# Chunk-selected attention with top-1 routing: the order of TensorE's work in a head pair, and three score units on column tiles

## The chip, the cores and the metric

The kernel runs on one core of a Trainium2 chip. The metric is the device time of one execution in microseconds. The kernel before takes 360.15 us (median of three runs, 359.7 to 360.66). The engines are TensorE (PE; its weight loads are listed as PEld), VectorE (DVE), ScalarE (ACT), GpSimd (POOL) and SyncE (SP). TensorE reads SBUF and writes PSUM.

## The reference, cut to what matters

Attention over 4 batches of 8 heads, 768 positions and a head width of 64, in which every query attends only to its 6 best key chunks of 32 (and causally), followed by a layer of 8 experts in which every token goes to one expert.

```python
k_chunks = k.reshape(B, H, nc, chunk, D)              # nc = 24 chunks of 32 keys
k_min, k_max = np.min(k_chunks, axis=3), np.max(k_chunks, axis=3)
ub = np.sum(np.maximum(q[:, :, :, None, :] * k_min[:, :, None, :, :],
                       q[:, :, :, None, :] * k_max[:, :, None, :, :]), axis=-1)
ub = np.where(causal, ub, -1e9)
top_chunks = np.argsort(ub, axis=-1)[..., -6:]        # the selection
scores = scale * np.matmul(q, k.transpose(0, 1, 3, 2))
mask = sel & (pos[:, None] >= pos[None, :])           # sel: the key's chunk is among top_chunks
attn = softmax(np.where(mask, scores, -1e9))
x = attn @ v                                          # heads side by side: (3072, 512)

logits = x @ w_gate                                   # 8 experts
expert_idx = np.argmax(logits, axis=1)
out[token] = gate * (relu(x[token] @ w1[e]) @ w2[e])  # e = expert_idx[token]
```

The sum of the larger products is q·(k_max + k_min)/2 + |q|·(k_max − k_min)/2, so the kernel computes the bound by two matmuls, without the halves (the order stays the same).

## The kernel before

The kernel goes through 16 head pairs `i` (4 in a batch). Two heads are worked on together, side by side in the 128 partitions. For a pair, `prep_steps` transposes keys and queries, takes the smallest and largest of each key chunk, and makes the bounds, the selection and the mask rows, which are appended to the queries (`QSB`, rows 64 to 87) so that the score matmul adds -50 for every chunk not selected. The steps of pair i+1 and i+2 run inside pair i.

```python
def k_half(hf):                                   # hf: first or second half of the keys
    pt = ps_m.tile([128, 384], FP32, tag="m")
    for t in range(3):
        nc.tensor.transpose(pt[:, ts(t, 128)], s["k"][:, 3 * hf + t], ident_f[:])
    pk = pt[:].rearrange("p (c w) -> p c w", w=CH)
    nc.vector.tensor_reduce(s["kmx"][:, ts(hf, 12)], pk, AX.X, ALU.max)
    nc.vector.tensor_reduce(s["kmn"][:, ts(hf, 12)], pk, AX.X, ALU.min)
    nc.scalar.activation(kte[0:64, 0, ts(hf, 384)], pt[0:64, :], AF.Copy, bias=0.0, scale=0.125)
    nc.scalar.activation(kte[0:64, 1, ts(hf, 384)], pt[64:128, :], AF.Copy, bias=0.0, scale=0.125)
# q_t(hf): three transposes; q_e(hf): VectorE copy qT, ScalarE |q| (qA) and QSB of head 1
def kse():                                        # key sums and differences, block by head
    for hd in range(2):
        r = slice(64 * hd, 64 * hd + 64)
        c = slice(32 * hd, 32 * hd + NCH)
        nc.vector.tensor_tensor(ks[r, c], s["kmx"][r, :], s["kmn"][r, :], ALU.add)
        nc.vector.tensor_tensor(kd[r, c], s["kmx"][r, :], s["kmn"][r, :], ALU.subtract)
def ub():                                         # bounds: column tiles of 64
    for w_, nm in ((ks, "qT"), (kd, "qA")):
        for h in range(2):
            nc.tensor.matmul(pu[64 * h:64 * h + 64, 0:320], lhsT=w_[:], rhs=..., ...)
    nc.scalar.activation(s["ubT"][:, 0:320], pu[:, 0:320], AF.Copy)
# select(): three transposes of ubT, then on VectorE ubm, twelve MAX8, nsel
# mask():   six transposes of nsel into 64 partitions, two ScalarE copies into QSB
```

The scores of a pair come in seven units: 0 and 1 for the first half of the queries, 2 to 6 for the second. Unit 1 and unit 6 have two parts, 256 and 128 queries wide, the others one of 384. A score tile takes two PSUM banks, and there are two of them. The exponentials `P` go to the attention-times-V (AV) matmuls, which use column tiles of 64 (a head each), and are added up on VectorE for the softmax's denominator.

```python
ps_m = tc.alloc_tile_pool(name="ps_m", bufs=3, space=PSUM)   # transposes, bounds, sums
ps_s = tc.alloc_tile_pool(name="ps_s", bufs=2, space=PSUM)   # scores, 2 banks each
ps_o = tc.alloc_tile_pool(name="ps_o", bufs=1, space=PSUM)   # AV output

def scores(i, u):
    ...
    for n, (kb, w, c0) in enumerate(parts):
        for hd in range(2):
            nc.tensor.matmul(pv[:, hd, :], lhsT=kte[:, hd, ts(kb, 128)],      # 128 columns
                             rhs=qsb[:, hd, ds(qb * 384 + 384 - w, w)], ...)
    for pv, (kb, w, c0) in zip(pvs, parts):
        nc.scalar.activation(P[:, :, ds(c0, w)], pv, AF.Exp)                  # one for each part
    # affine_select on GpSimd for the diagonal blocks

def attend(i, u):
    if first: s["po"] = ps_o.tile([128, 384], FP32, tag="o", name="po")
    for n, (kb, w, c0) in enumerate(parts):
        for hd in range(2):
            nc.tensor.matmul(po[64 * hd:64 * hd + 64, 384 - w:384], lhsT=vt[:, kb, hd, :],
                             rhs=P[:, hd, ds(c0, w)], ...)
    if last:
        nc.vector.tensor_copy(out=ot[:], in_=po[:])
    # and on VectorE: acc += P, except for the first unit
```

The router's part of a pair: `ud` (column tiles of 32: the denominators and the logits), `lgp` (transposes of it, reciprocal, division), `x0` and `x1` (transposes of the outputs `ot`, scaling into rows). Once in a batch the tokens are ranked (`rank`). The program order of a pair is also the order of TensorE, GpSimd and SyncE; the order of VectorE and ScalarE inside the loop is picked by the compiler, with program order as the priority.

```python
for g in range(4):
    if g == 0:   scores(i, 2); scores(i, 3); run(rout, i - 2, "x1")
    elif g == 1: scores(i, 4); scores(i, 5)
                 if hp == 1 and b > 0: route[b - 1][1]()            # rank
                 run(prep, i + 1, "select")
    elif g == 2: scores(i, 6); run(prep, i + 2, "k0"); run(prep, i + 1, "mask")
    else:        run(rout, i - 1, "lgp", "x0")
                 scores(i + 1, 0); scores(i + 1, 1)
                 run(prep, i + 2, "k1", "q0", "q0e", "q1")
    for u in groups[g]: attend(i, u)          # groups = (0, 1), (2, 3), (4, 5), (6,)
    if g == 3: run(prep, i + 2, "q1e", "kse")
    if g == 0: run(prep, i + 1, "ub")
    if g == 1: run(rout, i - 1, "ud")
```

## Time and profile before

| what | value |
|---|---|
| time, median of three runs | 360.15 us |
| profiled execution, span | 358.6 us |
| first pair's preparation | to 16.6 us |
| loop, first score matmul of pair 0 to that of pair 15 | 16.58 to 230.70 us |
| a regular pair | 13.66 us |
| a pair that ranks a batch | 15.65 us |
| first expert matmul | 243.13 us |

Times in the profile are microseconds from the start of the span. "L298" is line 298 of the kernel. `128*64` behind a matmul is the part of the array that its weights take: 128 rows, 64 columns. An fp32 matmul shows as two instructions with the same shape, a bf16 one as one. TensorE's ends are modelled, so what counts is where the next group starts. "<-" names what ended a wait; "issue" means that nothing in the profile held the engine.

### The profile page before, as it was taken

What the parts mean: (1) busy time and instruction counts of PE and PEld (TensorE: products, weight loads), DVE (VectorE), ACT (ScalarE), POOL (GpSimd) and SP (SyncE); (2) the same over time, 40 slices, a digit from 0 to 9 for tenths busy, and PEclk for the clock granted to TensorE, in tenths of its full rate; (3) what the DMA queues carried; (4) which work ended last, traced back from release to release, by engine and by line L of the source; (5) the groups of instructions that cost most, each with busy time, mean ns of one, the idle gap of its engine ahead of it and who ended that gap; (6) DMA issues with size and microseconds to landing.
All of it is one profiled execution on the core that took longest, in us unless ns stands there. A gap on an engine that the chain in (4) does not pass through costs nothing. (4 is left out here: it accounts for less than half of the span.)

```text
span 358.6 us, 7585 instructions
## 1 busy us (share of the span) xinstructions
PE 326.9 (91%) x2312; PEld 171.5 (48%) x2312; DVE 235.0 (66%) x815; ACT 231.2 (64%) x398; POOL 180.4 (50%) x296
## 2 busy tenths in 40 slices
PE   6679999999899999999999988998799999999990
PEld 5535455455455465554554545443344344444430
DVE  5799889889999898999988999846460000000000
ACT  2497797797687897867977967642344444445440
POOL 3075425445474453466534547575577665653331
PEclk9999999999999999999999999999999999999996
DMA  8619998999957999937989973476999999998851
GB/s 153 112 26 194 210 220 139 215 167 215 207 127 151 182 176 195 202 100 178 200 134 212 187 148 113 73 135 116 165 211 233 221 237 197 203 186 201 157 126 48
DMA packets 138215, 59.83 MB, mean 167 GB/s; under 512 B 122811, under 2 KB 131005, under 8 KB 138176
## 3 DMA queue, kind: packets, MB, share of 16 engines
q1 hardware_dynamic: 119072, 29.52, 45.4%
q0 software_dynamic: 17536, 29.42, 42.0%
q10 hardware_dynamic: 1568, 0.39, 0.6%
q8 instruction: 21, 0.34, 0.4%
q14 instruction: 18, 0.15, 0.2%
HBM read 56.14 MB, written 10.51 MB: 186 GB/s over the span
## 5 line engine op out<-in xcount | busy, mean ns | idle before, releaser
L332 DVE TENSOR_TENSOR Pa<-Pa,Pr 128x768 f32<-128x768 f32 (+2 forms) x112 | 81.6, 729 | 1.1
L307 POOL TENSOR_SCALAR_AFFINE_SELECT Pr<-Pr 128x256 f32<-128x256 f32 x80 | 33.5, 437 | 67.3 <-ACT Pr L303 66.1
L303 ACT ACTIVATE Pr<-ps 128x768 f32<-128x768 f32 (+2 forms) x112 | 65.0, 630 | 3.2 <-PE ps L298 2.9
L612 PE MATMUL py<-w_all,hT 128*128 x224 | 52.7, 379 | 2.7 <-DMA hT<-h__3653 1.9
L298 PE MATMUL ps<-QSB,KTE 128*128 128x384 bf16 (+2 forms) x288 | 50.4, 292 | 1.2 <-DVE QSB L711 0.2
L620 POOL DMA_INDIRECT out_dram<-y,ti_all x28 | 27.8, 993 | 30.2 <-ACT y L619 26.3
L298 PEld LDWEIGHTS <-KTE 128*128 128x128 bf16 x288 | 24.1, 97 | 27.3 <-issue 21.2
L612 PEld LDWEIGHTS <-hT 128*128 128x128 bf16 x224 | 21.8, 98 | 29.5 <-DMA hT<-h__3653 2.3
L619 ACT ACTIVATE y<-py,gt_all 128x512 f32<-128x512 f32 x27 | 18.6, 687 | 20.8 <-PE py L612 18.4
L454 POOL DMA_INDIRECT xs_dram<-xrow,sli x24 | 26.9, 1121 | 7.7 <-issue 5.0
L356 ACT ACTIVATE ud<-pu 128x384 f32<-128x384 f32 x16 | 7.9, 492 | 32.8 <-PE pu L353 30.7
L303 ACT ACTIVATE Pa<-ps 128x768 f32<-128x768 f32 x32 | 26.0, 812 | 3.8 <-PE ps L298 3.2
L601 PE MATMUL ph<-w_all,KTE 128*128 x120 | 28.4, 379 | 0.0
L169 POOL DMA_DIRECT2D w_all<-in_moe_w_dram x32 | 24.3, 760 | 0.0
L307 POOL TENSOR_SCALAR_AFFINE_SELECT Pa<-Pa 128x256 f32<-128x256 f32 x16 | 6.4, 398 | 35.3 <-ACT Pa L303 35.3
L601 PE MATMUL ph<-w_all,QSB 128*128 x96 | 22.7, 379 | 0.3 <-issue 0.3
L575 DVE TENSOR_TENSOR ti_all<-xgqA,inv_i 128x1 int32<-128x1 int32 x9 | 1.4, 159 | 29.6 <-DMA xgqA<-xs_dram,grow 29.6
L554 POOL DMA_INDIRECT xgqA<-xs_dram,grow x14 | 14.6, 1046 | 10.2 <-issue 3.3
L554 POOL DMA_INDIRECT xgqT<-xs_dram,grow x14 | 14.5, 1033 | 8.7 <-DVE gt_all L577 4.9
L325 DVE COPY ot<-po 128x384 f32<-128x384 f32 x32 | 17.7, 553 | 1.6 <-PE po L320 0.9
L575 DVE TENSOR_TENSOR ti_all<-xgqT,inv_i 128x1 int32<-128x1 int32 x8 | 1.3, 159 | 26.5 <-DMA xgqT<-xs_dram,grow 26.5
L226 POOL CAST QSB<-qT 64x384 bf16<-64x384 f32 x30 | 16.3, 551 | 4.1 <-DVE qT L224 2.8
(311 smaller groups left out, 665.0 us busy)
## 6 DMA issues: line engine op xcount, KB each, us to landing
w_all<-in_moe_w_dram POOLq DMA_DIRECT2D x32, 512.0 KB, 6.0
out_dram<-y,ti_all POOLq DMA_INDIRECT x28, 3.6
t__122<-in_k_dram SPq DMA_DIRECT2D x2, 192.0 KB, 3.5
t__125<-in_q_dram ACTq DMA_DIRECT2D x2, 192.0 KB, 4.0
t__128<-in_v_dram SPq DMA_DIRECT2D x2, 192.0 KB
t__196<-in_k_dram SPq DMA_DIRECT2D x2, 192.0 KB, 3.1
t__206<-in_q_dram SPq DMA_DIRECT2D x2, 192.0 KB, 3.8
t__209<-in_v_dram SPq DMA_DIRECT2D x2, 192.0 KB
```

The costliest lines, as they stand in the source:

```text
L169: nc.gpsimd.dma_start(out=dst, in_=src.rearrange("(c p) f -> p c f", p=128))
L298: nc.tensor.matmul(pv[:, hd, :], lhsT=kte[:, hd, ts(kb, 128)], rhs=qsb[:, hd, ds(qb * 384 + 384 - w, w)], start=True, stop=True, skip_grou ...
L303: nc.scalar.activation(P[:, :, ds(c0, w)], pv, AF.Exp)
L307: nc.gpsimd.affine_select(out=pd, in_=pd, pattern=[[0, 2], [1, 128]], compare_op=ALU.is_ge, fill=0.0, base=0, channel_multiplier=-1)
L325: nc.vector.tensor_copy(out=ot[:], in_=po[:])
L332: nc.vector.tensor_tensor(acc[:, :, 384 - w:384], acc[:, :, 384 - w:384], P[:, :, ds(c0, w)], ALU.add)
L454: d = nc.gpsimd.indirect_dma_start(out=xs_dram[:], out_offset=bass.IndirectOffsetOnAxis(ap=sli[:, u:u + 1], axis=0), in_=bst[b][f"xrow{u % ...
L554: d = nc.gpsimd.indirect_dma_start(out=xg_bufs[j % XB].bitcast(I32), out_offset=None, in_=xs_dram[:], in_offset=bass.IndirectOffsetOnAxis( ...
L601: nc.tensor.matmul(ph[:, fh, :], lhsT=xT[:, c, :], rhs=w_all[:, ds(wo + (c * F + fh * 512), 512)], start=(c == 0), stop=(c == NDC - 1), sk ...
L612: nc.tensor.matmul(py[:], lhsT=hT[:, c, :], rhs=w_all[:, ds(wo + (W1W + c * DM), DM)], start=(c == 0), stop=(c == NFC - 1))
L619: nc.scalar.activation(y[:], py[:], AF.Copy, bias=0.0, scale=fs[j]["gt"])
L620: d = nc.gpsimd.indirect_dma_start(out=out[:], out_offset=bass.IndirectOffsetOnAxis(ap=fs[j]["ti"], axis=0), in_=y[:], in_offset=None, bou ...
```

## The change

TensorE's work in a pair is regrouped by the part of the array that it uses. Work on the full array (128*128) is to be done in two visits for each pair instead of four; all else goes on column tiles. For this, score units 2, 3 and 6, which stand between column-tiled work, are split over two column tiles of 64 keys each; the row transposes `x1` and the first key transposes `k0` move next to the selection's. To allow it, each step is taken apart into its TensorE (`_mm`), VectorE (`_v`) and ScalarE (`_a`) parts. With it come three smaller edits: the exponentials of a two-part unit become one instruction (the score tile is now laid out by head), the key sums and differences are made for both heads at once and multiplied by a 0/1 mask `bm` into one tile `KSD`, and the ranking's gate values are split from its logits.

```diff
-        def kse():
-            for hd in range(2):
-                r = slice(64 * hd, 64 * hd + 64)
-                c = slice(32 * hd, 32 * hd + NCH)
-                nc.vector.tensor_tensor(ks[r, c], s["kmx"][r, :], s["kmn"][r, :], ALU.add)
-                nc.vector.tensor_tensor(kd[r, c], s["kmx"][r, :], s["kmn"][r, :], ALU.subtract)
+        def kse():
+            kt2 = work.tile([128, 2, NCH], FP32, tag="top8", name="kt2")
+            nc.vector.tensor_tensor(kt2[:, 0], s["kmx"][:], s["kmn"][:], ALU.add)
+            nc.vector.tensor_tensor(kt2[:, 1], s["kmx"][:], s["kmn"][:], ALU.subtract)
+            nc.vector.tensor_tensor(ksd[:, :, :, 0:NCH], kt2[:].unsqueeze(2).to_broadcast([128, 2, 2, NCH]),
+                                    bm[:].unsqueeze(1).to_broadcast([128, 2, 2, NCH]), ALU.mult)
 ...
-    def scores(i, u):
+    def scores(i, u, split=False):
         ps = ps_s.tile([128, 2, 512], FP32, tag="s", name="ps")
+        n = 64 if split else 128
+        for kb, w, c0 in parts:
+            for hd in range(2):
+                for h in range(128 // n):
+                    nc.tensor.matmul(ps[ds(h * n, n), hd, ds(c0, w)], lhsT=kte[:, hd, ds(kb * 128 + h * n, n)],
+                                     rhs=qsb[:, hd, ds(qb * 384 + 384 - w, w)],
+                                     start=True, stop=True, skip_group_check=True)
-        for pv, (kb, w, c0) in zip(pvs, parts):
-            nc.scalar.activation(P[:, :, ds(c0, w)], pv, AF.Exp)
+        nc.scalar.activation(P[:], ps[:, :, 0:384], AF.Exp)
 ...                                      # the loop; n = i + 1, m = i + 2
                 if g == 0:
-                    scores(i, 2)
-                    scores(i, 3)
-                    run(rout, i - 2, "x1")
+                    scores(i, 2, True)
+                    scores(i, 3, True)
+                    av(i, 0)
+                    av(i, 1)
+                    o_ev(i, 0)
+                    add(i, 1)
+                    run(prep, n, "ub")
                 elif g == 1:
                     scores(i, 4)
                     scores(i, 5)
-                    if hp == 1 and b > 0:
-                        route[b - 1][1]()
-                    run(prep, i + 1, "select")
+                    run(prep, n, "sel_mm")
+                    run(rout, i - 2, "x_mm", 1)
+                    run(prep, m, "k_mm", 0)
+                    if router:
+                        rank_mm()
+                    run(prep, n, "sel_v")
+                    if router:
+                        rank_v()
+                    run(rout, i - 2, "x_v", 1)
+                    run(prep, m, "k_v", 0)
+                    run(prep, m, "k_a", 0)
+                    av(i, 2)
+                    av(i, 3)
+                    add(i, 3)
+                    run(rout, i - 1, "ud")
                 elif g == 2:
-                    scores(i, 6)
-                    run(prep, i + 2, "k0")
-                    run(prep, i + 1, "mask")
+                    scores(i, 6, True)
+                    run(prep, n, "mask")
+                    av(i, 4)
+                    av(i, 5)
+                    add(i, 4)
+                    add(i, 5)
                 else:
-                    run(rout, i - 1, "lgp", "x0")
-                    if i + 1 < NP:
-                        scores(i + 1, 0)
-                        scores(i + 1, 1)
-                    run(prep, i + 2, "k1", "q0", "q0e", "q1")
+                    run(rout, i - 1, "lgp_mm")
+                    run(rout, i - 1, "x_mm", 0)
+                    if n < NP:
+                        scores(n, 0)
+                        scores(n, 1)
+                    run(rout, i - 1, "lgp_v")
+                    run(rout, i - 1, "x_v", 0)
+                    run(prep, m, "k_mm", 1)
+                    run(prep, m, "k_v", 1)
+                    run(prep, m, "k_a", 1)
+                    for hf in range(2):
+                        run(prep, m, "q_mm", hf)
+                        run(prep, m, "q_v", hf)
+                        run(prep, m, "q_a", hf)
+                    av(i, 6)
+                    o_ev(i, 1)
+                    add(i, 6)
+                    run(prep, m, "kse")
```

`av`, `o_ev` and `add` are the three parts of `attend`: the matmuls, the copy of the output, the add. The pools keep their buffers: three for `ps_m`, two for `ps_s`, one for `ps_o`.

## The prediction

> **What bounds the kernel now.** I read the page's busy times first, then the busy time of each engine per head pair, then the waits in the steady stretch from 100 to 200 us, then TensorE's own timeline for one pair.
>
> ```profile
> span 358.6 us, 7585 instructions
> PE 326.9 (91%) x2312; PEld 171.5 (48%) x2312; DVE 235.0 (66%) x815; ACT 231.2 (64%) x398; POOL 180.4 (50%) x296
> ```
>
> The second half of the span is the expert stage, and the change doesn't touch it. So the 66% of VectorE is an average over two different stages. The attention loop has to be read by itself, in stretches that run from one pair's first score matmul to the next pair's (columns: stretch, its length, then busy time and count of PE, PEld, DVE, ACT, POOL, granted clock, DMA share, GB/s):
>
> ```profile
> 115.42:129.08 13.66, 13.58 (x110) 7.45 (x108) 12.62 (x40) 11.36 (x22) 5.57 (x12) 1.00 1.00 167
> 129.08:142.74 13.66, 13.58 (x110) 7.45 (x108) 12.62 (x40) 11.36 (x22) 6.32 (x13) 1.00 1.20 198
> 142.74:158.39 15.65, 14.24 (x122) 7.74 (x120) 15.06 (x58) 11.78 (x24) 8.33 (x14) 1.00 0.85 166
> ```
>
> A regular pair takes 13.66 us, equal to the last digit from pair to pair. A pair that also ranks a batch's tokens takes 15.65 us, and there are three of those. In a regular pair TensorE is never seen idle, while VectorE has about 1.0 us free, ScalarE 2.3 us and GpSimd over 7 us. In a ranking pair VectorE has 0.6 us free and is the bound. The waits in the stretch:
>
> ```profile
> ACT ud L356 <- PE pu L353: 12.0, 6, 2.7
> PEld L298 <- issue: 8.8, 28, 0.5
> PEld po L320 <- issue: 7.0, 40, 0.2
> DVE ubm L251 <- PE pt L249: 4.5, 6, 0.9
> PEld pu L241 <- ACT qA L225: 1.3, 5, 0.3
> ```
>
> VectorE and ScalarE wait for TensorE (0.75 and 2 us in a pair). TensorE's weight loads wait mostly for "issue", which means for nothing that the trace shows. So TensorE sets the pace of a regular pair, with VectorE close behind. The timeline tells what "issue" is:
>
> ```profile
> 130.98 0.87 PE L320 MATMUL po<-Pr,t__1666 128*64 128x256 f32 x8
> 131.78 0.82 PE L298 MATMUL ps<-QSB,KTE 128*128 128x384 bf16 x4
> 132.50 0.55 PE L386 MATMUL pt<-ident_f,ot 128*128 128x128 f32 x3
> 132.98 0.87 PE L320 MATMUL po<-Pa,t__1869 128*64 128x384 f32 x4
> 133.68 0.82 PE L320 MATMUL po<-Pr,t__1869 128*64 128x256 f32 x8
> 134.32 0.71 PE L241 MATMUL pu<-qT,KS 128*64 128x320 f32 x4
> 134.86 0.71 PE L241 MATMUL pu<-qA,KD 128*64 128x320 f32 x4
> 135.50 1.06 PE L298 MATMUL ps<-QSB,KTE 128*128 128x384 bf16 x4
> 136.41 0.55 PE L249 MATMUL pt<-ident_f,ubT 128*128 128x128 f32 x3
> ...
> 142.36 0.55 PE L386 MATMUL pt<-ident_f,ot 128*128 128x128 f32 x3
> 142.74 0.82 PE L298 MATMUL ps<-QSB,KTE 128*128 128x384 bf16 x6
> ```
>
> Read starts, not durations: ends of matmuls are modelled. The four qT matmuls and the four qA matmuls are the same work. The first group hands over to another 128*64 group after 0.54 us, the second to a 128*128 group after 0.64. Three row transposes take 0.38 us (142.36 to 142.74) ahead of 128*128 work and 0.48 (132.50 to 132.98) ahead of 128*64 work. So **a change of tile shape costs about 0.10 us**. The attention-times-V group of eight takes 0.80 us (130.98) with a switch on either side and 0.64 (133.68) with none.
>
> **What the Trainium skill says.** "TensorEngine Tiling (Array Packing)", Key Properties: changing the tiling mode, not just the tile, drains the engine. The trace agrees, with 0.10 us for each change. The same page, Restrictions, says that column tiling disables fast weight load. The split scores lose it; but the mask transposes, with 64-column bf16 loads, start 0.06 us apart here (six within 0.36), so I expect their loads to stay hidden behind matmuls of 0.16 us. "TensorE: Matmul & The Clock Gate", its first table: VectorE's and ScalarE's queues are strict FIFO, so an op that TensorE needs waits behind whatever was queued ahead of it. That matters below.
>
> **Part 1, the visits.** Counted in program order, a pair now changes shape nine times: scores and x1 (full), AV and bounds (64), scores and select (full), AV (64), sums (32), score 6 and first keys (full), mask and AV (64), rows, scores and transposes (full), AV (64). Afterwards it is six: scores 4, 5 with select, x1 and first keys (full), AV (64), sums (32), score 6 split with mask and AV (64), rows, scores and transposes (full), AV with scores 2, 3 split and AV and bounds (64). Three changes fewer at 0.10 us: **-0.30 us a pair**. The slow first load after a switch (0.37 against 0.32 us between the first two AV starts) goes with them, another -0.05 or so.
>
> **Part 2, the split.** Units 2, 3 and 6 get 8 more matmuls and 8 more loads. Two column tiles run side by side: in the AV groups the partner starts 0.007 us later. A score of 384 columns stays at 0.16 us. The 128-wide part of unit 6 takes 0.056 us and has two loads to hide: **0 to +0.1 us**.
>
> **Part 3, the moved transposes.** x1 (0.38 us without its switch) and the first keys (0.34) are moved, not removed: 0 for TensorE. What moves with them is 0.98 us of ScalarE copies (two of 0.49), 0.93 us of VectorE reductions and 0.47 us of row scaling, out of the crowded stretch ahead of the bounds and into the one after the selection, where ScalarE now waits 1.9 us for the sums. In that stretch the last score unit (the 1.06 at 135.50, where 0.82 is usual) waits 0.24 us for its score buffer, behind ScalarE's queue. That should mostly go: **-0.1 to -0.24**.
>
> **Part 4, smaller things.** The key sums: now two groups whose means are 0.347 and 0.289 us, two of each in a pair, 0.88 us from start to start where I followed them. Then two short ops (0.17) and one of 96 elements (0.25, as the 96-element lgt product takes here): -0.3 us of VectorE. The exponentials of units 1 and 6: 0.59 + 0.39 become one of 0.81, -0.17 each on ScalarE, off the path.
>
> TensorE's own sum: 13.66 - 0.35 - 0.17 + 0.05 = **13.2 us**.
>
> **Part 5, what takes some back.** There is one PSUM tile for the output (the pool `ps_o` has one buffer). The last AV of a pair fills it, VectorE copies it out, the next pair's first AV overwrites it. Today two score units and x1 (0.72 + 0.48 us) lie between. Afterwards only two split units, about 0.65 and no switch. The copy needs about 0.27 us for the last matmul to end, 0.05 for the signal, 0.56 for the copy and 0.1 for the signal back: 0.98 us from the last AV start, against about 0.75 until TensorE is there. **+0.2 us at least**, even if VectorE takes it up at once. In the new program order both query copies (0.47 each) stand ahead of it, where one stood behind it until now; if VectorE keeps them so, +0.5. Then comes the loop through VectorE. From the start of the selection to the end of the key sums VectorE works without a gap; 12.62 - 0.3 less the output copy and the add of unit 1 (0.47 + 1.0) leaves 10.85 us. From there the bounds (1.15), scores (0.67), selection transposes (0.38) and two signals (0.3) bring it to the next selection: 10.85 + 2.5 = **13.35 us**. I take 13.35 us for a regular pair, -0.3.
>
> **Ranking pairs** are bound by VectorE (15.06 of 15.65). The 0.3 us of the key sums come off, and the rank matmuls, today ahead of the selection's and waiting 0.54 us for their operand, go behind it: -0.5 each.
>
> **Sum.** 12 regular intervals x 0.3 + 3 ranking x 0.5 = 5.1 us. The first pair (16.6 us, with the constants for the key sums on GpSimd) and the expert stage, which starts when the loop ends, keep their length. 360.15 - 5.1 = **355.0 us**.
>
> **Rivals.**
> 1. *The switches are the gain and nothing takes their place*: 13.1 us a pair and 1.0 off a ranking pair, 15 x 0.55 + 1.2, about 350.5 us. For it: VectorE has 1.0 us free. Against: that time lies in one gap ahead of the selection, and the output copy isn't in it.
> 2. *The output copy and VectorE's order become the wait*: the copy is taken up one or two ops late (0.47 to 0.93), and the pair ends at 13.6 to 13.9 us: 359 to 363. For it: VectorE ran without a gap up to the output copy in the pair that I followed. Against: work is taken out ahead of it (0.93 of reductions).
> 3. *DMA becomes the bound*, since the share is already 1.0 to 1.2 in regular pairs: no gain, 359 to 360. Against: no engine waits for a transfer between 100 and 200 us, and keys and queries are loaded two pairs ahead.
>
> **Range and chances.** My number lies between rivals 1 and 2. The range 351.0 to 360.5 takes in most of rival 1 and half of rival 2. Over 2% faster means under 352.9, so 0.48 us off every pair, nearly all of rival 1: 0.22. Over 2% slower means over 367, nearly half a microsecond added to every pair: 0.08. Within 2%: 0.70.
>
> **What would show it.** Right: bounds-to-split-scores without "issue" loads and six changes a pair; split scores 0.16 us per pair of tiles; a new wait of TensorE for the output copy ahead of unit 0's AV, some 0.2 us; regular pairs at 13.2 to 13.5 us; ranking pairs near 15.1; expert stage unchanged in length. Wrong: split scores at twice the time (loads exposed), which adds 0.9 us a pair; the output copy late by an op or more; or the mask waiting for the selection because row scaling and key reductions went ahead of it on VectorE.

## The result, and the profile after

The changed kernel takes 378.72 us (median of four runs, 378.21 to 380.27), the kernel before 359.92 us on the same chip (358.9 to 360.66). The ratio is 1.053, with a 95% interval of 1.049 to 1.057. The change made the kernel 5% slower; the prediction was 1.4% faster. In the profiled executions 377.3 us stand against 358.6: **18.7 us to explain**.

The head of the page, and the busy times of stretches that run from one pair's first score matmul to the next pair's (columns as before). First a regular pair, then a ranking pair, then pair 0:

```profile
span 377.3 us, 7736 instructions
PE 331.9 (88%) x2430; PEld 180.4 (48%) x2440; DVE 240.1 (64%) x799; ACT 228.9 (61%) x366; POOL 188.7 (50%) x297
```

```profile
125.78:140.99 15.21, 13.87 (x117) 7.87 (x117) 13.07 (x39) 11.24 (x20) 6.15 (x13) 1.00 1.00 159
156.19:171.89 15.70, 14.43 (x128) 8.37 (x128) 14.77 (x55) 11.40 (x21) 8.00 (x15) 1.00 0.84 157
17.47:35.15 17.68, 12.46 (x86) 6.88 (x87) 13.61 (x42) 11.16 (x20) 8.29 (x22) 0.90 0.42 75
```

A regular pair takes 15.20 us instead of 13.66, and there are seven such intervals (10.8 us in all). Pair 0 takes 17.68 instead of 14.40 (+3.3). The two pairs that follow a ranking pair take +1.4 and +1.1, the loop starts 0.9 us later (it scatters by more than that from run to run), the last interval is 0.9 longer, and pair 1 0.1. Ranking pairs are as long as before (+0.05 each), and from the start of the last pair to the end it is 127.98 us against 127.88. These sum to 18.7.

No engine is full now. TensorE and VectorE both stand still for more than a microsecond in a pair. The waits of the loop from 100 to 200 us (us in total, times, longest):

```profile
ACT ud L365 <- PE pu L362: 21.4, 7, 3.3
...
DVE ubm L264 <- PE pt L258: 6.5, 5, 1.6
...
PE ps L303 <- ACT QSB L285: 3.2, 10, 0.4
...
PE po L329 <- DVE ot L341: 1.4, 4, 0.4
```

Each of TensorE, VectorE and ScalarE waits for another of the three. Such a ring of waits has no single bound; one has to walk around it. TensorE's timeline of the regular pair, its waits in brackets:

```profile
126.50 0.65 PE L303 MATMUL ps<-QSB,KTE 128*128 128x384 bf16 x5 [0.40 <-ACT QSB L285]
...
128.29 0.87 PE L329 MATMUL po<-Pr,t__1463 128*64 128x256 f32 x8
128.99 0.82 PE L303 MATMUL ps<-QSB,KTE 128*64 128x384 bf16 x8
130.18 0.87 PE L329 MATMUL po<-Pa,t__1700 128*64 128x384 f32 x4 [0.37 <-POOL lg L391]
...
134.10 0.49 PE L400 MATMUL px<-ident_f,ot 128*128 128x128 f32 x3
134.43 0.49 PE L205 MATMUL pk<-ident_f,t__1855 128*128 128x128 f32 x3
135.28 0.87 PE L329 MATMUL po<-Pa,t__1700 128*64 128x384 f32 x4 [0.36 <-DVE ot L341]
...
140.29 0.49 PE L400 MATMUL px<-ident_f,ot 128*128 128x128 f32 x3
140.99 0.32 PE L303 MATMUL ps<-QSB,KTE 128*128 128x384 bf16 x1 [0.21 <-ACT QSB L285]
```

Compare each gap between starts with the same gap where nothing waited. The next pair's scores lose 0.37 (head 0) and 0.56 us (head 1, 0.72 from start to start instead of 0.16): the mask rows are copied late. The first AV loses 0.54, the AV after the selection 0.43, the bounds 0.19, the last score unit 0.15. That is 2.24 us, so TensorE's own work is 15.20 - 2.24 = **13.0 us**. The work shrank as predicted, and waits took the room. The "POOL lg" at the first AV is a name to be careful with: the output copy on VectorE ended 0.1 us before that AV started (130.08), and an experiment below moves the AV with the copy.

VectorE from the end of one pair through the selection to the key sums, in the kernel before; the prediction judged this stretch by busy time alone:

```profile
121.59 0.55 DVE L325 COPY ot<-po 128x384 f32<-128x384 f32 x1
...
123.33 0.46 DVE L251 TENSOR_TENSOR ubm<-pt,cbias 128x288 f32<-128x288 f32 x1 [0.86 <-PE pt L249]
123.83 1.12 DVE L259 MAX8 top<-ubm 128x8 f32<-128x24 f32 x12
...
133.97 0.17 DVE L234 TENSOR_TENSOR KD<-kmx,kmn 64x24 f32<-64x24 f32 x1
```

And after:

```profile
134.31 0.46 DVE L264 TENSOR_TENSOR ubm<-pt,cbias 128x288 f32<-128x288 f32 x1 [1.64 <-PE pt L258]
134.68 0.55 DVE L341 COPY ot<-po 128x384 f32<-128x384 f32 x1
135.14 1.10 DVE L272 MAX8 top<-ubm 128x8 f32<-128x24 f32 x12
136.17 0.54 DVE L405 TENSOR_TENSOR xrow<-px,rec 128x384 bf16<-128x384 f32 x1
...
137.46 0.54 DVE L211 TENSOR_REDUCE kmn<-pk 128x12 f32<-128x384 f32 x1
137.92 3.07 DVE L337 TENSOR_TENSOR Pa<-Pa,Pr 128x768 f32<-128x768 f32 x3
...
146.47 0.26 DVE L223 TENSOR_TENSOR KSD<-kt,bm 128x96 f32<-128x96 f32 x1
```

Look at the output copy. Before, it ran at 121.59, ahead of the selection, in the time in which VectorE waits for the bounds. After, it runs behind the selection's first op, and in front of it VectorE is idle for 1.64 us. The copy writes a tile `ot` (three buffers, two used in a pair), and the buffer it needs is still read by the x1 transposes of the pair before last. They now run at 134.10 on TensorE, behind the selection's transposes; the last AV into the output had started at about 131.5, some 3 us ahead of the copy. So the copy waits for x1, falls into VectorE's full stretch, and the AV that overwrites the output waits for the copy. From selection to the end of the key sums it was 10.81 us; now it is **12.43**. The rest of the ring is 2.85 and 2.77 us: 13.66 and 15.20.

The list of the difference, from start to start: output copy +0.46, x1's row scaling +0.46 (before it came after the key sums), the three long adds 2.99 instead of 2.72, reciprocal and first part of the add of unit 6 1.17 instead of 0.69, the second part of that add 0.67 instead of 0.46, key sums 0.78 instead of 0.87, query copies -0.14, the selection's first op -0.13.

ScalarE around its one long gap:

```profile
138.03 0.49 ACT L365 ACTIVATE ud<-pu 128x384 f32<-128x384 f32 x1 [2.95 <-PE pu L362]
138.41 0.97 ACT L216 ACTIVATE KTE<-pk 64x384 bf16<-64x384 f32 x2
...
140.24 1.41 ACT L285 ACTIVATE QSB<-pm 24x640 bf16<-24x640 bf16 x2
```

The first-key copies were meant for this gap of 2.95 us. They come after it, because VectorE's reductions of the same keys end at 138.0 and the program has them first. So they stand ahead of the last exponential and of the mask copies, for which the next pair's scores wait.

Pair 0 has a wait of its own:

```profile
29.76 0.88 PE L205 MATMUL pk<-ident_f,t__385 128*128 128x128 f32 x3 [3.12 <-DMA t__385<-in_k_dram]
```

The key transposes of pair 2 now come with the selection of pair 1, at 26.5 us, but those keys are issued at 25.83 and land at 29.7.

### The profile page after: what moved, and what is told of

It reads as the page before. It is cut to its first block, busy times and chain, and to the rows that moved or that the text cites. A ratio compares the mean times of both kernels' runs of the same rounds, so it can differ in the third digit from the quotient of the medians.

```text
span 377.3 us, 7736 instructions
## 1 busy us (share of the span) xinstructions
PE 331.9 (88%) x2430; PEld 180.4 (48%) x2440; DVE 240.1 (64%) x799; ACT 228.9 (61%) x366; POOL 188.7 (50%) x297
## 5 line engine op out<-in xcount | busy, mean ns | idle before, releaser
L337 DVE TENSOR_TENSOR Pa<-Pa,Pr 128x768 f32<-128x768 f32 (+2 forms) x112 | 89.4, 798 | 7.3 <-POOL Pr L316 1.9
L316 POOL TENSOR_SCALAR_AFFINE_SELECT Pr<-Pr 128x256 f32<-128x256 f32 x80 | 43.0, 556 | 97.3 <-ACT Pr L312 97.2
L312 ACT ACTIVATE Pr<-ps 128x768 f32<-128x768 f32 x80 | 63.1, 815 | 2.2 <-PE ps L303 2.0
L303 PE MATMUL ps<-QSB,KTE 128*64 128x384 bf16 (+5 forms) x416 | 52.3, 291 | 8.9 <-ACT QSB L285 7.4
L303 PEld LDWEIGHTS <-KTE 128*64 128x64 bf16 (+1 forms) x416 | 27.2, 105 | 35.6 <-issue 31.2
L216 ACT ACTIVATE KTE<-pk 64x384 bf16<-64x384 f32 x60 | 29.0, 483 | 13.0 <-DVE kmn L211 10.6
L478 POOL DMA_INDIRECT xs_dram<-xrow,sli x24 | 24.7, 1030 | 12.3 <-DVE sli L471 7.1
L285 ACT ACTIVATE QSB<-pm 24x640 bf16<-24x640 bf16 x30 | 20.8, 693 | 0.7
L210 DVE TENSOR_REDUCE kmx<-pk 128x12 f32<-128x384 f32 x32 | 17.5, 547 | 5.4 <-PE pk L205 5.4
L578 POOL DMA_INDIRECT xgqA<-xs_dram,grow x14 | 14.4, 1029 | 11.1 <-issue 4.6
```

The costliest lines, as they stand in the source:

```text
L216: nc.scalar.activation(kte[0:64, hd, ts(hf, 384)], pt[64 * hd:64 * hd + 64, :], AF.Copy, bias=0.0, scale=0.125)
L285: nc.scalar.activation(qsb[64:64 + NCH, hd, 128:S], pt[32 * hd:32 * hd + NCH, 128:S], AF.Copy)
L303: nc.tensor.matmul(ps[ds(h * n, n), hd, ds(c0, w)], lhsT=kte[:, hd, ds(kb * 128 + h * n, n)], rhs=qsb[:, hd, ds(qb * 384 + 384 - w, w)], s ...
L312: nc.scalar.activation(P[:], ps[:, :, 0:384], AF.Exp)
L316: nc.gpsimd.affine_select(out=pd, in_=pd, pattern=[[0, 2], [1, 128]], compare_op=ALU.is_ge, fill=0.0, base=0, channel_multiplier=-1)
L337: nc.vector.tensor_tensor(acc[:, :, 384 - w:384], acc[:, :, 384 - w:384], P[:, :, ds(c0, w)], ALU.add)
```

## The experiments

The theory after this reading: *x1's new place keeps the output copy back and lengthens the ring through VectorE; the first keys' new place delays the mask copies; pair 0 waits for its keys*. The rival: *the split score units, or the shape changes, cost more than they seem*. A second rival came up on the way: *VectorE has too much work, whatever the order*. The kernel before took between 359.9 and 367.9 us on the four chips used, so each experiment is told as its ratio to the kernel before on its own chip (the change itself: 1.053), with the length of a regular pair from its profile (13.66 before, 15.20 after). The pair is the firmer figure: from the last pair's start to the end, where the edits change little, the profiled runs take anything from 125.8 to 134.9 us, and the ratio carries that too.

### First round: the changed kernel with one thing moved

**e1: x1 one step earlier**, next to x0.

```diff
-   run(rout, i - 2, "x_mm", 1)      # g == 1, behind the selection's transposes
-   run(rout, i - 2, "x_v", 1)
+   run(rout, i - 1, "x_mm", 1)      # g == 3, behind x_mm 0
+   run(rout, i - 1, "x_v", 1)
```

> The second row transposes (x1) go next to the first ones (x0), into the other full-array visit, one step earlier than in the changed kernel; still six changes of shape a pair. Theory (three waits made by the new order): x1 reads the output tile that VectorE's next output copy has to overwrite, so that copy, and with it AV of unit 2, waits for x1. With x1 earlier, the start of unit 2's AV goes from 0.63 us after the last transpose to 0.20, VectorE's idle gap ahead of the selection shrinks from 1.6 to about 1.2 us, and the regular pair from 15.2 to 14.7 to 15.0 us: 371 to 376 us in all against 378.7. Rival 1 (the split scores cost the time): 378 to 379, no change. Rival 2 (a loop through VectorE and ScalarE sets the pace and one wait only hands on to another): 377 to 380.

Measured: 1.079 (1.072 to 1.086), but a regular pair of 14.60, 0.60 shorter. VectorE's stretch fell to 11.75 us, and the AV after the selection no longer waits. The total is worse, mostly because pairs 6 and 10, behind ranking pairs, take 18.8 and 19.9 us. The waits of 100 to 140 us name it:

```profile
PE pq L232 <- DVE xrow L405: 3.0, 1, 3.0
DVE xrow L405 <- DMA xs_dram<-xrow,sli: 3.0, 1, 3.0
```

A row scaling that comes earlier writes into a row buffer whose old content is still being scattered. So x1's place is worth 0.6 us a pair, and this new place isn't free either.

**e2: the first keys' reductions and copies ahead of the selection's vector work.**

```diff
+   run(prep, m, "k_v", 0); run(prep, m, "k_a", 0)
    run(prep, n, "sel_v")
...
-   run(prep, m, "k_v", 0); run(prep, m, "k_a", 0)
```

> VectorE's reductions of the first key half come ahead of the selection's twelve MAX8, not behind them, so ScalarE can copy the keys while it waits for the sums. Nothing else is moved. Theory: ScalarE's two key copies (0.98 us) no longer stand between the sums and the mask copies; the first score of the next pair no longer waits for the mask copies (0.37 + 0.56 us now), regular pair 14.3 to 14.7 us, 366 to 373 us in all. The selection ends 0.9 us later, which the mask transposes (1.2 us of room) should not feel. Rival 1 (split scores): no change. Rival 2 (loop): under 0.3 us a pair, over 374.

Measured: 1.048 (1.043 to 1.052), a pair of 14.87. The waits for the mask copies (-0.93) and at the bounds (-0.19) are gone, but about 0.6 appears at the query transposes and 0.2 more at the last score unit. The waits at both AVs stay at 0.54 and 0.43. The theory's second part holds; a third of its size comes out at the end of the ring.

**e3: the second query copy behind the output copy**, as it was before.

```diff
-   run(prep, m, "q_mm", 1); run(prep, m, "q_v", 1); run(prep, m, "q_a", 1)
+   run(prep, m, "q_mm", 1)
    av(i, 6); o_ev(i, 1)
+   run(prep, m, "q_v", 1); run(prep, m, "q_a", 1)
```

> VectorE's copy of the second query half is put behind the output copy at the end of a pair, as it stood before the change. Theory: unit 0's AV now waits 0.54 us for the output copy, 0.46 of it for that query copy; so the wait falls to about 0.1 to 0.2 us, but the key sums come no earlier and the bounds wait (0.15 now) takes over up to half: 0.2 to 0.4 us a pair, 373 to 376 us. Rival 1 (split scores): no change. Rival 2 (loop): no change, the bounds wait grows by what the AV wait loses.

Measured: 1.066 (1.061 to 1.070), a pair of 15.53. The first AV starts 0.38 us behind the last split score instead of 0.70, so the output copy is what it waits for, whatever name the profile prints. But the bounds then wait for the key sums:

```profile
133.71 0.76 PE L249 MATMUL pu<-qT,KSD 128*64 128x320 f32 x4 [0.79 <-DVE KSD L223]
```

A wait taken away in one place came back larger in another: VectorE's order is the limit, not that one op.

**e4: no split of units 2, 3 and 6.**

```diff
-   scores(i, 2, True); scores(i, 3, True)      # and scores(i, 6, True)
+   scores(i, 2); scores(i, 3)                  # and scores(i, 6)
```

> Units 2, 3 and 6 use the full array again; everything else as in the changed kernel, so a pair has nine or more changes of shape. Theory (waits): the split costs nothing (its tile pairs start 0.156 us apart, as full scores do at 0.16); undoing it adds up to 0.3 us of switches to TensorE's own work, part of which falls into waits that are there anyway: 378 to 383 us. Rival 1 (the split scores cost the time, by loads without the fast path and 8 more matmuls): 362 to 372 us. Rival 2 (loop): 378 to 380.

Measured: 1.044 (1.039 to 1.049), a pair of 14.93. There are more changes of shape, and yet the pair is 0.27 us shorter. So the changes of shape aren't on the path of the changed kernel at all, and the split brings nothing there. Why it is somewhat faster without isn't settled; VectorE's stretch is 12.20 us instead of 12.43.

### Second round: how much is VectorE, how much x1

**e5: one add less.** The add of unit 4 is left out of the changed kernel, so the softmax's denominators lack that unit. It takes about 1 us out of VectorE's stretch.

```diff
    av(i, 4); av(i, 5)
-   add(i, 4)
    add(i, 5)
```

> The changed kernel without the VectorE add of unit 4's exponentials (the softmax denominators lack that unit: work is left out, nothing else is changed). Theory now: a loop through VectorE sets the pace of the changed kernel: from the start of the selection to the end of the key sums VectorE works without a gap (12.4 us), then bounds, scores and selection transposes on TensorE bring it to the next selection (2.8 us). The add takes 1.05 us of the first part, so the regular pair falls from 15.2 to 14.0 to 14.4 us and the time to 364 to 369 us. Rival (TensorE's own waits for mask copies and output copies set the pace, and VectorE only follows): an add that TensorE does not wait for gives under 0.3 us a pair, 374 to 379 us.

Measured: 1.044 (1.040 to 1.048), a pair of 15.18: nothing gained in a regular pair, and the loop as a whole is no shorter, so the ratio isn't a gain of this edit. The add of unit 6 now waits where it had almost not waited:

```profile
140.66 0.87 DVE L337 TENSOR_TENSOR Pa<-Pa,Pr 128x512 f32<-128x512 f32 x1 [0.80 <-POOL Pr L316]
```

GpSimd's masking of unit 6 follows ScalarE's exponential, which stands behind the denominators' copy and the key copies. So VectorE's amount of work alone is not the bound, and the second rival in its plain form fell. Two rings of nearly equal length, one through VectorE and one through ScalarE's queue, hold the pair together.

**e6: the same add left out of the kernel before.**

```diff
-        else:
+        elif u != 4:
             acc = s[f"acc{qb}"]
```

> The same add left out of the kernel before (the denominators lack unit 4). There the same loop is 10.8 + 2.85 = 13.66 us, just the pair's length, while TensorE alone needs 13.4 (13.66 less the 0.24 wait of unit 5). Theory (loop sets the pace of the changed kernel, TensorE that of the kernel before, the two being close): a regular pair falls by 0 to 0.25 us at most, ranking pairs by up to 0.9: 355 to 360 us. Rival (the kernel before was bound by VectorE's loop as well, and TensorE not at all): 0.6 us or more a pair, under 352 us.

Measured: 0.989 (0.985 to 0.993), a pair of 13.60 (-0.06); the loop as a whole is 1.5 us shorter, and the rest of the ratio lies outside it. The kernel before was bound by TensorE in a regular pair, as the prediction had it.

**e7: x1 ahead of score unit 4**, and the add of unit 6 behind the key sums.

```diff
+   run(rout, i - 2, "x_mm", 1); run(rout, i - 2, "x_v", 1)
    scores(i, 4); scores(i, 5)
    run(prep, n, "sel_mm")
-   run(rout, i - 2, "x_mm", 1)         # and x_v 1 further down
...
-   add(i, 6)
    run(prep, m, "kse")
+   add(i, 6)
```

> In the changed kernel the second row transposes (x1) open the full-array visit, ahead of scores 4 and 5, where they stood behind the selection's; and the add of unit 6 comes behind the key sums. So the copy of the first output (0.46 us, held up until now because x1 reads the tile that it overwrites), the row scaling of x1 (0.46) and a part of the add (0.3 to 0.6) leave the loop for VectorE's idle gap ahead of the selection. Theory (loop): 12.4 less 1.4 = 11.0 of VectorE, and 2.8 + 0.4 for x1 on TensorE: regular pair 13.8 to 14.3 us, 360 to 367 us in all. Rival (mask copies and first output copy set the pace): these waits stay, 14.8 us or more, over 372.

Measured: 1.039 (1.032 to 1.046), pairs of 14.1 to 14.6, a little longer than expected. What stays: 0.43 us at the scores of head 1, 0.2 at the query transposes, 0.54 at the first AV.

**e8: x1 where it was before**, units 2 and 3 whole again, unit 6 split, first keys moved, the add of unit 6 behind the key sums.

```diff
-   scores(i, 2, True); scores(i, 3, True)
+   scores(i, 2); scores(i, 3)
+   run(rout, i - 2, "x_mm", 1); run(rout, i - 2, "x_v", 1)
```

> In the changed kernel x1 is put back between scores 3 and AV of unit 0, with scores 2 and 3 on the full array again (eight changes of shape a pair); only the first keys stay with the selection and only unit 6 is split; the add of unit 6 is behind the key sums. Theory (loop): the same 1.4 us leave VectorE's loop and TensorE's part of it stays 2.8: 13.5 to 14.0 us a regular pair, 357 to 363 us; the 0.54 us wait of unit 0's AV goes too, since x1 gives VectorE time for the copy. Rival (changes of shape decide): two more changes than in the changed kernel, so no better than the run with x1 in front.

Measured: 1.034 (1.031 to 1.038), pairs of 14.1 to 14.9, longer than expected. With x1 elsewhere (e1, e7, e8) a regular pair is 0.3 to 1.1 us shorter than in the changed kernel; in e7 and e8 the later add of unit 6 has a part in it.

### Third round: both rings, the parts on the kernel before, the load

**e9: first keys ahead (e2) and one add less (e5, without the add of unit 4) together.**

```diff
+   run(prep, m, "k_v", 0); run(prep, m, "k_a", 0)
    run(prep, n, "sel_v")
...
-   add(i, 4)
```

> Both edits that gave little alone: the key reductions ahead of the twelve MAX8, and the add of unit 4 left out (the denominators lack that unit). Theory now: from one selection to the next two branches of nearly the same length run side by side in the changed kernel, one through VectorE's queue (12.4 + 2.8 us), one through ScalarE's (key copies, exponential of unit 6, mask copies, then scores, query transposes, first AV, bounds on TensorE), so shortening one hands the pace to the other. Both shortened together: 13.8 to 14.3 us a regular pair, and 1.00 to 1.03 of the kernel before. Rival (something common to both, such as first AV and second AV waiting for output copies, sets the pace): no lower than the better of the two alone, 14.87.

Measured: 1.031 (1.025 to 1.037), a pair of 14.68, longer than expected. Both reliefs give 0.52 us together, and then 0.54 and 0.43 at the AVs hold it, which neither touches: the ring now goes from the selection to the end of the output copy (10.45 us), then by the first AV, the bounds and the scores back to the selection (4.23).

**e10: x1 moved, and nothing else, in the kernel before.**

```diff
     scores(i, 3)
-    run(rout, i - 2, "x1")
 ...
     run(prep, i + 1, "select")
+    run(rout, i - 2, "x1")
```

> The kernel before with one thing of the change alone: x1 goes from its place ahead of AV of unit 0 to behind the selection's transposes. Theory: x1 reads the output tile that the next output copy overwrites, so that copy (0.47 us) and x1's row scaling (0.47) move from VectorE's gap ahead of the selection into its full stretch behind it: 10.8 + 0.9 + 2.7 us, a regular pair of 14.1 to 14.6 us in place of 13.66, ratio 1.02 to 1.04. Rival (moving x1 by itself does no harm, it saves TensorE a change of shape and a stop): 13.5 to 13.7 us, ratio 0.99 to 1.0.

Measured: 1.028 (1.023 to 1.034), a pair of 14.75: **+1.09 us from one line that moves no more than three transposes and a row scaling**. The AV behind the selection on TensorE, then VectorE (the x1 transposes start at 128.89):

```profile
130.07 0.87 PE L320 MATMUL po<-Pa,t__1661 128*64 128x384 f32 x4 [0.69 <-DVE ot L325]
```

```profile
129.09 0.46 DVE L251 TENSOR_TENSOR ubm<-pt,cbias 128x288 f32<-128x288 f32 x1 [1.60 <-PE pt L249]
129.46 0.55 DVE L325 COPY ot<-po 128x384 f32<-128x384 f32 x1
```

It is the picture of the changed kernel: the output copy behind the selection's first op, 1.60 us of idle VectorE in front, the AV waiting for the copy. VectorE's stretch went from 10.81 to 11.90 us, the same +1.09 as the pair: 0.47 for the output copy, 0.46 for x1's row scaling, 0.27 because the long adds now follow one another directly, less 0.13 at the selection's first op. This is the largest single part. No run moves the transposes without the row scaling, so the division is the trace's and not an experiment's.

**e11: the keys of pair 2 loaded earlier** (changed kernel, ahead of the late constants on GpSimd).

```diff
-   consts_last()
    load(2, "k", "q")
+   consts_last()
```

> In the changed kernel the loads of pair 2's keys and queries are issued ahead of the two small router-weight loads, which wait for GpSimd's constants on the same queue. Theory: in pair 0 TensorE waits 3.1 us for these keys, because their transposes now come with the selection, one group of steps earlier than before; with the early issue the first interval falls from 17.7 to 14.2 to 14.8 us, regular pairs stay at 15.2, so 3 us less in all: ratio 1.042 to 1.047. Rival (pair 0 is long for its other waits, constants on GpSimd among them): the first interval stays over 16.5.

Measured: 1.042 (1.034 to 1.050). Pair 0 fell from 17.68 to 14.56 us (-3.1), a regular pair stayed at 15.20. The cause of pair 0's loss is confirmed.

**e12: all mended**: x1 ahead of unit 4 and the add of unit 6 late (e7), first keys ahead (e2), keys loaded early (e11).

```diff
+   run(rout, i - 2, "x_mm", 1); run(rout, i - 2, "x_v", 1)
    scores(i, 4); scores(i, 5)
    run(prep, n, "sel_mm"); run(prep, m, "k_mm", 0)
+   run(prep, m, "k_v", 0); run(prep, m, "k_a", 0)
    run(prep, n, "sel_v")
...
    run(prep, m, "kse")
+   add(i, 6)                           # from ahead of it; load(2) as in e11
```

> The changed kernel with all that the runs point to: x1 at the head of the full-array visit, the key reductions ahead of the MAX8, the add of unit 6 behind the key sums, the early load. It keeps six changes of shape and the split scores. Theory: VectorE's branch 10.5 + 3.1, ScalarE's shorter by its key copies, TensorE's own work 13.05 plus the wait of the first AV for the output copy (0.5): regular pair 13.5 to 13.8, first interval 14.5, ranking pairs 15 to 15.5: ratio 0.99 to 1.01. If the six changes of shape were worth what was predicted and no wait were left: 13.1, ratio 0.97.

Measured: 1.015 (1.009 to 1.021), a pair of 14.27, ranking pairs 14.83, pair 0 15.41. The best version of the change, and still slower than the kernel before. Its waits:

```profile
124.59 0.87 PE L329 MATMUL po<-Pa,t__1700 128*64 128x384 f32 x4 [0.37 <-POOL lg L391]
...
132.41 0.47 PE L282 MATMUL pm<-ident_b,nsel 128*64 128x128 bf16 x5 [0.40 <-DVE nsel L275]
```

The first is the output copy again (starts 0.70 us apart instead of 0.16). The second is the one that the prediction named under "wrong": the mask waits because row scaling and key reductions went ahead of the selection on VectorE.

### Fourth round: the other parts alone, and what is left

**e13: the first key transposes moved, and nothing else, in the kernel before.**

```diff
     run(prep, i + 1, "select")
+    run(prep, i + 2, "k0")          # from behind scores(i, 6)
```

> The kernel before with the first key transposes, their reductions and copies behind the selection's transposes, and nothing else of the change. Theory: VectorE's stretch gets longer, since the reductions that stood between the three adds of units 3 to 5 are gone from there and each add now waits for the one before it (1.05 us from start to start where it was 0.87): 0.3 to 0.6 us a pair, 13.9 to 14.3, ratio 1.01 to 1.03. Rival (the move is good, since ScalarE's two copies fall into its idle time): 13.4 to 13.66, ratio 0.985 to 1.0.

Measured: 1.019 (1.014 to 1.023). Pairs of 13.9 to 14.5 us (+0.3 where they are steady), pair 0 17.8 (+3.4). A wait of some 0.4 us at the scores of head 1 is here too, and VectorE's stretch is 11.1 us instead of 10.8, as the theory had it.

**e14: the small edits alone** (one exponential for a two-part unit, key sums for both heads, the ranking's gate values split off and its matmuls behind the selection's), with x1, the first keys, the second query copy and the score units as before.

```diff
 # g == 1
-    route[b - 1][1]()
-    run(prep, i + 1, "select")
+    run(prep, n, "sel_mm")
+    rank_mm()                        # ranking pairs alone
+    run(prep, n, "sel_v")
+    rank_v()
 # and scores, kse and the gate values as in the changed kernel
```

> The changed kernel with x1, the first keys, the second query copy and all score units as they were before; what remains of the change are the joined exponentials, the key sums in one tile, the rank matmuls behind the selection and the gates split off. Theory: TensorE's own work is that of the kernel before, VectorE's stretch as well to 0.2 us: regular pair 13.4 to 13.8, ratio 0.99 to 1.005. Rival (the small edits carry part of the loss, by three dependent key-sum instructions): over 14.0, ratio over 1.015.

Measured: 1.003 (1.0003 to 1.0057). A ranking pair takes 13.97 us instead of 15.65 (-1.7), but the pairs behind the first two of them take 0.9 and 1.5 us more. A regular pair takes 13.92 (+0.26): the bounds start later, because the key sums end late (1.11 us from the AV's last group to the bounds, 0.65 before); x1's row scaling (0.47 us) now runs ahead of the last of them. Some other pairs are longer too (14.3 to 15.6), so that the sum is nil.

**e15: all mended and one add less** (the add of unit 4 left out, as in e5, so the denominators lack that unit).

```diff
 # e12, and
-   add(i, 4)
```

> The mended order without the add of unit 4 (the denominators lack that unit), to be held against the kernel before without the same add, whose regular pair took 13.60 us. Theory: the saved changes of shape are real (TensorE's own work 13.05 us) and hidden behind VectorE's stretch; with 1.05 us of VectorE gone the pair falls from 14.27 to 13.2 to 13.6, ratio 0.96 to 0.99. Rival (the first AV's wait for the output copy, 0.54, binds whatever VectorE does): 13.9 or more, ratio over 0.995.

Measured: 1.019 (1.014 to 1.025), a pair of 13.98, as the rival had it. With 1 us of VectorE's work removed it is still longer than before; 0.62 us at the output copy and 0.57 at the mask transposes stay, so TensorE's own work is 13.98 - 1.19 = 12.8 us.

**e16: all mended, with that add on GpSimd.**

```diff
+   add(i, 4, nc.gpsimd)             # eng.tensor_tensor(...), behind add(i, 5)
```

> The mended order with the add of unit 4 given to GpSimd (nothing left out); it comes behind VectorE's add of unit 5. GpSimd is idle 7 us in a pair. Theory: as with one add less, if the add doesn't disturb VectorE: 13.3 to 13.8 us, ratio 0.965 to 0.995. Rival (GpSimd takes long, so that the diagonal masks and the unit 6 add queue behind it, or it slows VectorE down while both read SBUF): 14.2 or more, ratio over 1.01.

Measured: 1.094 (1.089 to 1.098), a pair of 15.64. GpSimd's add takes 1.81 us; VectorE's next one behind it:

```profile
131.79 0.69 DVE L337 TENSOR_TENSOR Pa<-Pa,Pr 128x512 f32<-128x512 f32 x1 [2.44 <-POOL Pa L337]
```

The adds are one chain through the same sum, and GpSimd comes to its link only behind the masks of unit 6. Moving work off VectorE inside that chain lengthens it.

Not tried: a fourth `ot` buffer, which would let the output copy go early with x1 in its new place, and a second PSUM tile for the output. Both would test directly what the moved reader shows indirectly.

## Why the prediction was wrong

**What bounds the kernel before: right.** TensorE in a regular pair, with e6 gaining only 0.06 us from VectorE; VectorE in ranking pairs.

**Part 1, the visits: right.** The group of eight AVs takes 0.70 us with one switch less (128.29 to 128.99), where it took 0.80; TensorE's own work is 13.0 us (12.8 in e15), predicted 13.2. The saving is real and off the path: e4 has more switches and is shorter.

**The drain and the queues: right.** The Trainium skill's "TensorEngine Tiling (Array Packing)", Key Properties, has the drain at a change of mode; 0.10 us each stood up. Its "TensorE: Matmul & The Clock Gate", first table, has strict FIFO queues on VectorE and ScalarE; the trace agrees, with ScalarE's key copies (138.41) run ahead of the mask copies (140.24) and 0.93 us lost at the scores.

**Part 2, the split: right.** In pair 0, where nothing waited behind them, the eight split score matmuls took 0.67 us to the next start (21.65 to 22.32); four whole ones at 0.16 make 0.64. The loads stay hidden.

**Part 3, the moved transposes: wrong in its sign, and the main failure.** The prediction said "0 for TensorE" and counted what moves with them as relief: out of the crowded stretch, into the one after the selection. It asked where the moved work would run, and didn't ask *what the moved work sets free*. x1 is the last reader of an `ot` tile; moved behind the selection, it holds the output copy back, and with its row scaling and the adds that then stand side by side it costs +1.09 us (e10). The first keys cost +0.3 (e13): their copies follow VectorE's reductions and so miss ScalarE's gap, and the long adds lose the reductions between them; which of the two sets the +0.3 isn't shown. "-0.1 to -0.24" for the last score unit came out as -0.10.

**Part 4, key sums: wrong by a factor of three.** -0.09 instead of -0.3 us. The 0.88 us of the old key sums hold one op that had collided (a 24-element op takes 0.17 us alone and 0.48 beside GpSimd's cast of the queries), while the new ones were set at their times alone (0.17, 0.17, 0.25). After the change one of them meets that cast: 0.48, and 0.78 in all.

**Part 5, the output tile: right.** +0.54 at the first AV (0.23 in e3, with one query copy back behind the output copy), where "+0.2 at least" and "if VectorE keeps them so, +0.5" stood.

**Part 5, the ring through VectorE: wrong.** Predicted 10.85 + 2.5 = 13.35, measured 12.43 + 2.77 = 15.20. The term that failed is 10.85 (of the 0.27 in the other, 0.15 is the wait of the last score unit). It was built from busy times, with the output copy subtracted as work that lies in the gap ahead of the selection. The copy stayed in (+0.47). Then come the key sums (+0.21 against the prediction), adds that follow one another directly (+0.27), the add of unit 6 behind GpSimd's mask (+0.48) and the second part of that add beside the casts (+0.21), less 0.14: 12.35 of 12.43. Busy time doesn't show the waits inside a stretch, and a stretch that is "without a gap" in one order has others in another.

**Ranking pairs: right in kind, hidden in effect.** -0.5 was predicted, +0.05 came. e14 shows -1.7 for the same edit without the two moves, though the pairs behind give much of it back. With the moves a ranking pair, 15.70 us, is only 0.5 longer than the ring of 15.2 makes a regular one.

**The first pair: wrong.** The preparation that was to keep its length ended at 17.47 us instead of 16.58, which shows little: with the same preparation the other runs of the changed kernel start the loop between 16.2 and 18.3. The interval of pair 0, counted among the regular ones, took +3.3 us. The prediction looked at transfers from 100 to 200 us, where keys lie two pairs ahead; in pair 0 they don't yet. e11 gives back 3.1. The expert stage kept its length, as predicted.

**The rivals.** Rival 2 had the mechanism in kind, output copy and VectorE's order, but put it at 13.6 to 13.9 us a pair. It meant the copy at the end of a pair, late by one or two ops; the one that x1 holds back is the copy in the middle of a pair, some 3 us late. Rivals 1 and 3 are out: TensorE waits, and no transfer holds the steady loop.

The parts taken alone on the kernel before, 1.09 + 0.3 + 0.26 = 1.65 us a pair, come near the 1.54 of all together, but that is in part luck: e10 and e13 both hold the 0.3 us of the adds, and the row scaling that delays e14's key sums stands elsewhere in the changed kernel. How much the two rings through VectorE and ScalarE each hold in the changed kernel is known only from e2, e5 and e9, and 0.27 us of e4 stays unexplained.

## What to carry to other kernels

Before you move a step, list the buffers that it is the last to read, and find who writes them next: the delay goes there, and it can be larger than everything the move saves. When an engine runs without a gap between two points of a loop, follow its order op by op from start to start in the new program; a sum of busy times is only a lower limit of that stretch. A saving on the engine that is busiest counts only if every ring of waits through the other engines is shorter than that engine's work.

## What the runs showed of the hardware

- An add of 128x768 fp32 on VectorE into the same sum starts the next op after 0.86 us when an independent op follows, and after 1.05 to 1.06 when the next add follows directly (kernel before 0.86 and 0.87; changed kernel, e2, e4, e13 1.05 and more). It was seen in several kernels and not measured by itself.
- GpSimd took 1.81 us for the add that VectorE does in 0.94.
- Small VectorE ops beside GpSimd: 0.17 us alone and 0.48 beside a cast of 64x384 (kernel before at 133.57, the changed kernel at 145.87). The Trainium skill's "SBUF — State Buffer", section "SBUF: two separate sides", has an exclusive lock between VectorE ops with two SBUF inputs and GpSimd ops that read SBUF; these numbers agree, and the prediction should have used it.
- Behind TensorE's wait of 3.12 us in pair 0 the granted clock was 0.50, from 29.70 to 32.60, and the first AV group there took about twice as long (1.34 us for four, against 0.70). In pair 0 of e11, without that wait, the clock was 1.00 throughout and the same group took 0.70.
